# Filling a permutation array: contiguous copies inside DRAM in place of 4-byte stores from SBUF

## The chip, the cores and the metric

The kernel runs on one core of a Trainium2 chip. The metric is the device time of one execution in microseconds, the median of several runs. Engines are named as in the profile: PE (TensorE), ACT (ScalarE), DVE (VectorE), POOL (GpSimd) and SP (SyncE). SP computes nothing here; its instruction stream, written SPq in the rows, issues most of the transfers, in order.

## The reference, cut to what matters

Three layers follow each other: linear attention with decay, a layer of routed experts, and a gated feed-forward. The middle one sends each of 3072 tokens to one of 8 experts:

```python
def _moe_ref(x, w_gate, w_output_gate, w1, w2):
    logits = x @ w_gate
    e_idx = np.argmax(logits, axis=1)
    ...
    for e in range(E):
        mask = e_idx == e
        h = np.maximum(x[mask] @ w1[e], 0.0)
        ye = h @ w2[e]
        out[mask] = gate_w[mask, None] * eom[mask, e, None] * ye
    return out.astype(np.float32)

def _moe2_ref(x, w_gate, w_val, w_out, rms_g):
    rms = np.sqrt(np.mean(x * x, axis=-1, keepdims=True) + 1e-06)
    xn = x / rms * rms_g
    g = xn @ w_gate
    silu = g * (1.0 / (1.0 + np.exp(-g)))
    val = xn @ w_val
    return (silu * val @ w_out).astype(np.float32)
```

Tokens are 512 wide, the experts' hidden width is 1024, that of the feed-forward 1536. `moe_w_output_gate` is scaled by 3.472.

## The kernel before, in words

**Attention and routing** go over 24 chunks of 128 tokens. For each token POOL writes its number with an indirect transfer into the DRAM array `lst`, which has a region of 3072 places for each expert (`place`, L577). The finished rows go to `xr` in DRAM.

**Experts.** The 8 experts are handled as 8 windows, in an order that the device works out from the counts. Window `w` takes up to `CAPS[w]` tokens (448, 456, 432, 416, 408, 400, 384, 368). Its list is read from `lst` into the SBUF tile `ix` as 128-partition columns and a remainder (`load_list`, L248 and L250). POOL gathers the rows by it into `xw` (L255), TensorE transposes them (`turn`, L271), and they are split into two parts that single passes carry, `xh` and `xl`. Eight steps `f` follow: `up` (L287) makes 128 hidden units; ACT writes them as `hh` (L293) and DVE what is left of them as `hl` (L294); one step later `down` (L300) adds their product to the output. The list, the gather and the transposes of window `w + 1` run inside window `w`.

**Weights** come in 64 tiles of 512 KB, one for each step of each window. SP loads a tile into one of three `raw` buffers (L183), ACT converts it (L179) and POOL writes the remainder (L180). The conversion runs up to 9 steps ahead of use, the load two tiles ahead of the conversion, from a table that is known only once the routing is done. The order on each engine is the order of the code: a manual schedule with no planner behind it.

**Permutation.** The rows of a window are computed side by side, so their results lie in the order of the windows in `z_dram`, of which there are two, so that the first blocks of the feed-forward can start before the last windows are done. Beside each of them stands an array `p_dram` with the token's number for each place. `ids` (L278, L280) fills it: in step 0 of window `w`, SP stores the columns of `ix` and the remainder, 4 bytes at a time, into array 0 and 1 for the first four windows (`both`) and into array 1 alone after that. A window writes `CAPS[w]` places; the next window overwrites what was too much, so the order of the stores matters. Two stores into the same array wait for each other. `load_perm` (L737) reads array 0 and array 1 back in the last window.

**Feed-forward.** In the last window SP also reads the first block of 384 columns from `z_dram` (L728), and weights `raw<-wm` (L205), which ACT and DVE decode from 64-bit words (L219 to L232). Twelve steps for each pair of blocks follow (`gate`, `project`), and POOL scatters the finished rows to the output by the permutation (L778).

Of the kernel before, what the change touches and what calls it, by code (L numbers as in the profile page):

```python
# [19 lines left out]
NT, DM = B * S, H * D  # L20
# [83 lines left out]
def fused_kernel(  # L104
# [26 lines left out]

# [1 line left out]
    stage = ctx.enter_context(ExitStack())  # L133
# [29 lines left out]

# [1 line left out]
    def wslot(t):  # L165
# [70 lines left out]

# [1 line left out]
    class Experts:  # L238
        """One window: up to n tokens of one expert."""

# [32 lines left out]

        def ids(self, w, n, pos, which):
            nt, rem = divmod(n, 128)
            t = ix[w % 2]
            for i in which:
                SP.dma_start(out=p_dram[i][bass.ds(pos, nt * 128)].rearrange("(t p) o -> p t o", p=128), in_=t[:, 0:nt])  # L278
                if rem:
                    SP.dma_start(out=p_dram[i][bass.ds(pos + nt * 128, rem)], in_=t[0:rem, nt])  # L280

# [31 lines left out]
        def evac_weighted(self, w, n):  # L313
            """The squares taken on the way, and the gain applied already."""
            self.ys = self.ys2[w % len(self.ys2)]
            for k in range(KB):
                p, y, g = ps[:, 4 + k, 0:n], self.ys[:, k, 0:n], gcol[:, k:k + 1]
                if k % 2:
                    DVE.tensor_scalar(out=y, in0=p, scalar1=g, scalar2=None, op0=ALU.mult)
                ACT.activation(out=self.sq[k][:, 0:n], in_=p, func=AF.Square)  # L320
                if k % 2 == 0:
                    ACT.activation(out=y, in_=p, func=AF.Copy, scale=g)  # L322
# [34 lines left out]
    regs = {}  # L357

    def wrow(w):
        if w == 0:  # L360
            return 0
        return SP.value_load(tab[0:1, TB_ROW + w:TB_ROW + w + 1], min_val=0, max_val=NE * NT - NT)

# [16 lines left out]
    def totals_c(room):  # L380
        """Where the windows' columns begin, and what of an expert's tokens is past its window."""
        nw = tf(TB_N)
# [22 lines left out]
        DVE.tensor_tensor(out=tabf[:, TB_FLAG:TB_FLAG + 1], in0=fl[:, 0:1], in1=fl[:, 1:2], op=ALU.add)  # L405
        # where a window leaves columns unwritten, the blocks read the first window's; they are redone at the end
        DVE.scalar_tensor_tensor(
# [4 lines left out]

# [1 line left out]
    with ExitStack() as es:  # L414
# [302 lines left out]

# [1 line left out]
    def w2(f, part, s, lo, hi):  # L719
# [79 lines left out]
    def settle(w, f, bank):  # L799
        """What is left of window w once its products are done, a step at a time."""  # L800
        n = CAPS[w]
        if f == 0:
            ex.square(0, n)
            ex.square(1, n)
        elif f == 1:
            ex.square(2, n)
            ex.square(3, n)
            ex.add(1, n, DVE)
        elif f == 2:
            ex.add(2, n, DVE)  # L810
            ex.add(3, n, DVE)
        elif f == 3:
            ex.halve(w, n, DVE)
        elif f == 4:
            ex.mean(w, n, bank)
            ex.inverse(0, n // 2)
        elif f == 5:
            ex.inverse(n // 2, n)
        elif f >= 6:
            for k in range(KB):  # L820
                if f == (6 + k // 2 if w < NE - 2 else 7):
                    ex.scale(k, n)

    for w in range(NE):
        n = CAPS[w]
        for f in range(NF):
# [7 lines left out]
            if w + 1 < NE:  # L834
                if f == 0:
                    ex.load_list(w + 1, CAPS[w + 1], wrow(w + 1))
                    if w == 0:
                        ex.load_list(0, n, 0)
                    ex.ids(w, n, wpos(w), both(w))
                elif f == 1:  # L840
                    ex.gather(w + 1, CAPS[w + 1])
                    if w == 0:
                        totals_c(sq[1][0:1])
                elif f in (5, 6):
                    ex.turn(w + 1, CAPS[w + 1], (2 * (f - 5), 2 * (f - 5) + 1))
            else:
                if f == 0:
                    ex.ids(w, n, wpos(w), both(w))
                    z_block(0, 0)
# [4 lines left out]
                elif f == 6:  # L854
                    load_perm(1, 0, NT // 128)
                    z_split(1, POOL)
            if w:
                settle(w - 1, f, 2 + f % 2)
# [5 lines left out]

    # the first two blocks of the feed-forward take over while the last window settles
    w = NE - 1
# [70 lines left out]

    # the last two blocks end apart, so that what the first returns is on its way before the second ends
    b0, b1 = NB - 2, NB - 1
# [16 lines left out]

# [1 line left out]
    def within(v, most):  # L958
# [11 lines left out]
    with tc.If(flag > 0):  # L970
        with ExitStack() as es:
# [5 lines left out]
            with tc.For_i(0, NE, 1) as w:  # L977
                pieces = nc.values_load(tab[0:1, bass.ds(w + TB_K, 1)], min_val=0, max_val=MAXP)
                with tc.For_i(0, pieces, 1) as i:
# [6 lines left out]
                    ex.turn(0, PIECE, range(KB))  # L986
                    ex.ids(0, PIECE, pos, (1,))
                    for f in range(NF):
# [78 lines left out]
```

## Time and profile before

| what | value |
|---|---|
| three runs | 1172.06, 1172.99 and 4084.11 us; median 1172.99 us |
| profiled execution, span from the first to the last instruction | 1170.0 us (the page gives no time of its own beside it) |
| TensorE busy, mean granted clock | 1070.0 us (91%), 0.968 |
| DVE, ACT, POOL busy | 538.5, 381.8, 338.9 us |
| transfers | 116.74 MB, of 53405 packets 18507 under 512 B |

The experts run from about 173 to 537 us; ahead of them lies attention, behind them the feed-forward. The clock of TensorE is given as a share of full speed: 1.00 is 2.4 GHz, 0.50 is 1.2 GHz. The third run is far from the other two, and the median does not rest on it.

### The profile page before, as it was taken

The page shows a single profiled execution, that of the slowest core. Times are in us where ns is not written, and L with a number is a line of the kernel's source. Part 1 is how long each engine was busy: PE and PEld are TensorE (multiplying, and loading weights), DVE is VectorE, ACT ScalarE, POOL GpSimd, SP SyncE. Part 2 cuts the span into 40 slices and gives each one's busy share as a digit, 9 for nine tenths or more (in the row PEclk, how much of TensorE's full clock was granted, in tenths as well). Part 3 has the DMA queues.
Part 4 walks back from the last instruction along what each step waited for, and adds up shares of the span by engine and source line. Part 5 has one row for each costly group of instructions (what it writes and reads, how often), then busy time and mean ns, then how long its engine had stood idle before and what let it go on. Part 6 is the DMA issues. An engine that isn't in the chain of part 4 may idle for free.

```text
span 1170.0 us, 16406 instructions
## 1 busy us (share of the span) xinstructions
PE 1070.0 (91%) x6393; PEld 993.8 (85%) x6394; DVE 538.5 (46%) x1045; ACT 381.8 (33%) x721; POOL 338.9 (29%) x271
## 2 busy tenths in 40 slices
PE   7787885979888999978989999999999999999996
PEld 6687765868788999978878889999999999999995
DVE  4699941235345556669888872111221112211111
ACT  1344430524324445445555542111221112211111
POOL 2355521644444656633343322000020000200002
PEclk9899978889998999989999999999999999999998
DMA  8999516452736656463334322000020000200001
GB/s 293 242 322 262 159 55 70 126 120 55 217 75 179 199 170 140 134 188 100 103 102 146 126 72 82 1 1 1 13 96 1 1 1 1 83 1 1 1 1 57
DMA packets 53405, 116.74 MB, mean 100 GB/s; under 512 B 18507, under 2 KB 30027, under 8 KB 50503
## 3 DMA queue, kind: packets, MB, share of 16 engines
q1 hardware_dynamic: 45142, 97.05, 28.6%
q0 software_dynamic: 4864, 12.53, 4.9%
q10 hardware_dynamic: 3312, 6.03, 1.5%
q8 instruction: 52, 0.85, 0.3%
q14 instruction: 35, 0.28, 0.1%
HBM read 93.04 MB, written 23.11 MB: 99 GB/s over the span
## 4 chain that ended last, share of the span: by engine, by line
issue 44%; DMA 12%; PE 12%; DVE 11%; POOL 5%; ACT 2%; SPq 2%; POOLq 0%; DVEq 0%; ACTq 0%
PE ps L300 5%; PE ps L287 5%; DMA raw<-wmoe 5%; DMA perm<-ix 4%; POOL w L180 3%; DVE fb L226 2%; DVE fb L229 2%; POOL out_dram L778 2%; DVE fu L232 1%; DVE fb L223 1%; DMA raw<-wm 1%; DMA out_dram<-ob,perm 1%; DVE a L753 1%; DVE al L755 1%; ACT ah L754 1%
## 5 line engine op out<-in xcount | busy, mean ns | idle before, releaser
L745 PE MATMUL ps<-zh,w 128*128 128x384 f32 x960 | 255.7, 337 | 1.3 <-ACT a L752 1.3
L753 DVE TENSOR_TENSOR a<-a,ps 128x384 f32<-128x384 f32 x96 | 52.9, 551 | 320.1 <-PE ps L745 315.5
L180 POOL TENSOR_TENSOR w<-raw,w 128x1024 fp32r<-128x1024 f32 x64 | 156.5, 2454 | 147.6 <-ACT w L179 146.8
L745 PEld LDWEIGHTS ps<-zh,w 128*128 128x128 f32 x960 | 175.3, 188 | 4.1 <-ACT a L752 1.7
L745 PE MATMUL ps<-xh,w 128*128 128x384 f32 x576 | 156.5, 341 | 9.9 <-ACT a L752 7.3
L745 PE MATMUL ps<-zl,w 128*128 128x384 f32 x480 | 161.6, 337 | 0.0
L300 PE MATMUL ps<-hh,w 128*128 128x448 f32 (+7 forms) x512 | 114.2, 368 | 40.4 <-ACT hh L293 40.4
L287 PE MATMUL ps<-xh,w 128*128 128x448 f32 (+7 forms) x512 | 150.9, 356 | 0.1
L763 PE MATMUL ps<-w,ah 128*128 128x512 f32 x564 | 145.4, 393 | 0.2 <-ACT ys L322 0.2
L300 PEld LDWEIGHTS ps<-hh,w 128*128 128x128 f32 x512 | 98.5, 199 | 46.2 <-ACT hh L293 42.9
L778 POOL DMA_INDIRECT out_dram<-xw,perm x10 | 9.9, 994 | 423.3 <-ACT xw L776 420.0
L745 PEld LDWEIGHTS ps<-xh,w 128*128 128x128 f32 x576 | 104.9, 188 | 17.4 <-ACT a L752 11.4
L763 PEld LDWEIGHTS ps<-w,ah 128*128 128x128 f32 x564 | 104.7, 188 | 16.6 <-ACT ys L322 0.6
L754 ACT ACTIVATE ah<-a 128x384 fp32r<-128x384 f32 x94 | 49.4, 525 | 209.9 <-DVE a L753 209.9
L752 ACT ACTIVATE a<-ps 128x384 f32<-128x384 f32 x96 | 46.8, 488 | 202.2 <-PE ps L745 202.2
L179 ACT ACTIVATE w<-raw 128x1024 fp32r<-128x1024 f32 x64 | 67.4, 1056 | 101.0 <-DMA raw<-wmoe 97.7
L287 PEld LDWEIGHTS ps<-xh,w 128*128 128x128 f32 x512 | 96.5, 190 | 3.6
L294 DVE SCALAR_TENSOR_TENSOR hl<-ps,hh 128x448 fp32r<-128x448 f32 (+7 forms) x64 | 37.5, 585 | 133.2 <-ACT hh L293 133.0
L745 PE MATMUL ps<-xl,w 128*128 128x384 f32 x288 | 96.9, 336 | 0.0
L745 PEld LDWEIGHTS ps<-zl,w 128*128 128x128 f32 x480 | 90.4, 188 | 2.3
L287 PE MATMUL ps<-xl,w 128*128 128x448 f32 (+7 forms) x256 | 90.4, 353 | 0.0
L180 POOL TENSOR_TENSOR w<-fu,w 128x512 fp32r<-128x512 f32 x36 | 55.8, 1549 | 111.3 <-ACT w L179 107.8
(154 smaller groups left out, 1520.8 us busy)
## 6 DMA issues: line engine op xcount, KB each, us to landing
raw<-wmoe SPq DMA_DIRECT2D x64, 512.0 KB
qkv<-att SPq DMA_DIRECT2D x22, 1024.0 KB
raw<-wm SPq DMA_DIRECT2D x36, 512.0 KB
xw<-z SPq DMA_DIRECT2D x8, 768.0 KB
xr<-row ACTq DMA_DIRECT2D x23, 256.0 KB
z<-ys SPq DMA_DIRECT2D x2, 912.0 KB
z<-ys SPq DMA_DIRECT2D x2, 896.0 KB
z<-ys SPq DMA_DIRECT2D x2, 864.0 KB
```

The lines of the kernel that those rows point to most:

```text
L179: ACT.activation(out=dst[:, 0, c], in_=src, func=AF.Copy)
L180: POOL.tensor_tensor(out=dst[:, 1, c], in0=src, in1=f32(dst[:, 0, c]), op=ALU.subtract)
L226: DVE.scalar_tensor_tensor(out=b, in0=lo, scalar=29, in1=b, op0=ALU.logical_shift_right, op1=ALU.bitwise_or)
L287: PE.matmul(p, lhsT=wtile[:, s, k * 128:(k + 1) * 128], rhs=x[w % len(xh)][:, k, 0:n], start=(i == 0), stop=(i == 3 * KB - 1),)
L294: DVE.scalar_tensor_tensor(out=hl, in0=p, scalar=0.0, in1=f32(hh), op0=ALU.max, op1=ALU.subtract)
L300: PE.matmul(ps[:, 4 + k, 0:n], lhsT=wtile[:, s, 512 + k * 128:512 + (k + 1) * 128], rhs=h, start=(f == 0 and j == 0), stop=(f == NF - 1 an ...
L745: PE.matmul(ps[:, part, 0:BT], lhsT=w2(f, part, s, k * 128, (k + 1) * 128), rhs=zz[:, k], start=(i == 0), stop=(i == 3 * KB - 1),)
L752: ACT.activation(out=a, in_=ps[:, 0, 0:BT], func=AF.Silu)
L753: DVE.tensor_tensor(out=a, in0=a, in1=ps[:, 1, 0:BT], op=ALU.mult)
L754: ACT.activation(out=ah, in_=a, func=AF.Copy)
L763: PE.matmul(ps[:, o_bank[b % 2][t]], lhsT=x[:, t * 128:(t + 1) * 128], rhs=w2(f, 2, s, 0, 512), start=(f == 0 and j == 0), stop=(f == NF2 ...
L778: ins = POOL.indirect_dma_start(out=out[:, :], out_offset=bass.IndirectOffsetOnAxis(ap=pm[:, t0 + t], axis=0), in_=o, in_offset=None, boun ...
```

## The change

`ids` no longer stores the SBUF tile. It copies `CAPS[w]` consecutive entries from the expert's region of `lst` to the permutation array, DRAM to DRAM, as one transfer. The call moves from step 0 of the window to step 3 (array 0) and step 5 (array 1). The second reading of window 0's list, which only the old store needed, is dropped. The row offset of a window is read from the table once and kept.

```diff
-        def ids(self, w, n, pos, which):
-            nt, rem = divmod(n, 128)
-            t = ix[w % 2]
-            for i in which:
-                SP.dma_start(out=p_dram[i][bass.ds(pos, nt * 128)].rearrange("(t p) o -> p t o", p=128), in_=t[:, 0:nt])
-                if rem:
-                    SP.dma_start(out=p_dram[i][bass.ds(pos + nt * 128, rem)], in_=t[0:rem, nt])
+        def ids(self, n, row0, pos, i):
+
+            SP.dma_start(
+                out=p_dram[i][bass.ds(pos, n)].rearrange("t o -> o t"), in_=lst[bass.ds(row0, n)].rearrange("t o -> o t")
+            )
...
+    rows_at = {}
+
     def wrow(w):
         if w == 0:
             return 0
-        return SP.value_load(tab[0:1, TB_ROW + w:TB_ROW + w + 1], min_val=0, max_val=NE * NT - NT)
+        if w not in rows_at:
+            rows_at[w] = SP.value_load(tab[0:1, TB_ROW + w:TB_ROW + w + 1], min_val=0, max_val=NE * NT - NT)
+        return rows_at[w]
...
                     ex.load_list(w + 1, CAPS[w + 1], wrow(w + 1))
-                    if w == 0:
-                        ex.load_list(0, n, 0)
-                    ex.ids(w, n, wpos(w), both(w))
...
                 if f == 0:
-                    ex.ids(w, n, wpos(w), both(w))
                     z_block(0, 0)
...
+            if f in (3, 5) and f // 4 in both(w):
+                ex.ids(n, wrow(w), wpos(w), f // 4)
```

The same call in the code for other shares of the experts, which does not run with these inputs, changes alike. PE, ACT, DVE and POOL keep their instructions and order; SP's stream goes from 469 to 447 rows.

SP's stream before, second window, step 0, after the two list loads. `perm_61` and `perm_62` are the two arrays in DRAM, `ix_102` the window's list, `raw_70` a weight buffer; `DMAHW` names are counters of landed transfers.

```order
L368 TENSOR_LOAD tab [waits DVE_49]
L368 ISA x2
L278 REGISTER_ALU
L278 DMA perm_61<-ix_102 128x3x1
L280 ISA
L280 DMA perm_61<-ix_102 72x1 [waits DMAHW2_49]
L278 REGISTER_ALU
L278 DMA perm_62<-ix_102 128x3x1
L280 ISA
L280 DMA perm_62<-ix_102 72x1 [waits DMAHW5_49,DMAHW4_49]
L183 ISA
L183 DMA raw_70<-wmoe 128x1024 [waits DMAHW6_49,Pool_49]
```

The same place after: the weight loads of steps 0 to 2 follow the list loads at once; these rows begin with the last of them.

```order
L183 DMA raw_69<-wmoe 128x1024 [waits DMAHW3_49,Pool_49]
L370 TENSOR_LOAD tab [waits DVE_49]
L370 ISA x2
L276 ISA
L276 DMA perm_61<-lst 12x38
L183 ISA
L183 DMA raw_70<-wmoe 128x1024 [waits DMAHW6_49,Pool_49]
L183 ISA
L183 DMA raw_68<-wmoe 128x1024 [waits DMAHW7_49,Pool_49]
L276 ISA
L276 DMA perm_62<-lst 12x38 [waits DMAHW4_49]
```

The four stores, two of which wait for the one before, have become two copies with weight loads ahead of and between them.

SP's stream before, last window, steps 0 and 1: the store, then the first block `z_59` of the feed-forward, a result store (`ys`) and three loads of feed-forward weights.

```order
L278 REGISTER_ALU
L278 DMA perm_62<-ix_102 128x2x1
L280 ISA
L280 DMA perm_62<-ix_102 112x1 [waits DMAHW5_49,DMAHW4_49]
L728 DMA xw<-z_59 128x4x384 [waits DMASW4_49,DMASW3_49,DMASW5_49,DMASW2_49,PE_49]
L355 REGISTER_ALU
L355 DMA z_60<-ys_1994 512x1x400 [waits DVE_49]
L205 DMA raw_69<-wm 128x1024 [waits DMAHW1_49,Pool_49]
L205 DMA raw_70<-wm 128x1024 [waits DMAHW2_49,Pool_49]
L205 DMA raw_68<-wm 128x1024 [waits DMAHW3_49,Pool_49]
```

The same place after, from the last load of expert weights on.

```order
L183 DMA raw_68<-wmoe 128x1024 [waits DMAHW3_49,Pool_49]
L730 DMA xw<-z_59 128x4x384 [waits DMASW4_49,DMASW5_49,DMASW3_49,DMAHW0_49,DMASW2_49,PE_49]
L353 REGISTER_ALU
L353 DMA z_60<-ys_1994 512x1x400 [waits DVE_49]
L205 DMA raw_69<-wm 128x1024 [waits DMAHW4_49,Pool_49]
L205 DMA raw_70<-wm 128x1024 [waits DMAHW6_49,Pool_49]
L205 DMA raw_68<-wm 128x1024 [waits DMAHW7_49,Pool_49]
```

The store has left this place. It stands, as a copy, at step 5 of the window, ahead of the full read of array 1 (`perm_104<-perm_62`):

```order
L370 TENSOR_LOAD tab
L370 ISA x2
L276 ISA
L276 DMA perm_62<-lst 16x23
L205 DMA raw_69<-wm 128x1024 [waits DMAHW7_49,DVE_49,Activation_49]
L739 DMA perm_104<-perm_62 128x24x1 [waits DMAHW2_49]
L205 DMA raw_70<-wm 128x1024 [waits DMAHW0_49,DMAHW5_49,DVE_49,Activation_49]
```

Before, seven loads of feed-forward weights and four other transfers stood between the store and that read; now one load does.

## Rows read from the trace of the kernel before

**Rows 1.** The page: span, busy time by engine, and the chain that ended last by line.

```profile
span 1170.0 us, 16406 instructions
...
PE 1070.0 (91%) x6393; PEld 993.8 (85%) x6394; DVE 538.5 (46%) x1045; ACT 381.8 (33%) x721; POOL 338.9 (29%) x271
...
PE ps L300 5%; PE ps L287 5%; DMA raw<-wmoe 5%; DMA perm<-ix 4%; POOL w L180 3%; DVE fb L226 2%; DVE fb L229 2%; POOL out_dram L778 2%; DVE fu L232 1%; DVE fb L223 1%; DMA raw<-wm 1%; DMA out_dram<-ob,perm 1%; DVE a L753 1%; DVE al L755 1%; ACT ah L754 1%
```

**Rows 2.** TensorE's waits from 170 to 600 us: who waited for whom, us, times, longest.

```profile
PE ps L300 <- ACT hh L293: 40.4, 7, 13.7
PE ps L300 <- DVE hl L294: 4.1, 3, 2.3
```

**Rows 3.** TensorE's timeline: start us, us, instruction, [idle before it, releaser].

```profile
206.47 3.35 PE L300 MATMUL ps<-hh,w 128*128 128x448 f32 x8 [13.68 <-ACT hh L293]
...
253.58 3.41 PE L300 MATMUL ps<-hh,w 128*128 128x456 f32 x8 [8.38 <-ACT hh L293]
...
303.82 3.25 PE L300 MATMUL ps<-hh,w 128*128 128x432 f32 x8 [5.10 <-ACT hh L293]
...
352.82 3.14 PE L300 MATMUL ps<-hh,w 128*128 128x416 f32 x8 [5.89 <-ACT hh L293]
...
511.03 2.82 PE L300 MATMUL ps<-hh,w 128*128 128x368 f32 x8 [4.81 <-ACT hh L293]
```

**Rows 4.** ACT's timeline in the second window, same columns.

```profile
252.03 1.06 ACT L179 ACTIVATE w<-raw 128x1024 fp32r<-128x1024 f32 x1 [15.29 <-DMA raw<-wmoe]
```

**Rows 5.** SyncE's queue (SPq) in the second window: start us, us, issue.

```profile
226.41 0.43 SPq L278 DMA_DIRECT2D perm<-ix  x1
...
235.59 0.39 SPq L278 DMA_DIRECT2D perm<-ix  x1
...
245.54 29.32 SPq L183 DMA_DIRECT2D raw<-wmoe  x8
```

**Rows 6.** The waits of SyncE's queue from 170 to 500 us.

```profile
SPq L280 <- DMA perm<-ix: 69.2, 9, 8.8
```

**Rows 7.** SyncE's queue in the fifth window.

```profile
378.16 0.42 SPq L278 DMA_DIRECT2D perm<-ix  x1
385.97 0.36 SPq L280 DMA_DIRECT2D perm<-ix  x1
```

**Rows 8.** Busy us by engine in the fifth window, TensorE's granted clock, DMA share, GB/s.

```profile
377.80:416.30 38.50, 38.50 (x210) 37.52 (x209) 21.24 (x24) 17.21 (x29) 23.81 (x12) 1.00 0.54 174
```

**Rows 9.** The same view of five stretches, each right after an idle of TensorE.

```profile
206.47:211.60 5.13, 5.13 (x14) 4.58 (x15) 1.23 (x2) 2.39 (x3) 5.13 (x3) 0.50 0.30 117
253.58:259.40 5.82, 5.82 (x15) 5.11 (x16) 5.68 (x5) 2.12 (x4) 4.68 (x2) 0.50 0.44 143
303.82:307.20 3.38, 3.38 (x9) 3.14 (x10) 3.10 (x3) 0.00 (x0) 1.98 (x1) 0.50 1.04 404
352.82:358.40 5.58, 5.58 (x16) 5.33 (x17) 3.10 (x3) 0.00 (x0) 2.03 (x1) 0.50 1.08 272
511.03:515.40 4.37, 4.37 (x14) 4.37 (x15) 4.23 (x6) 4.21 (x9) 3.93 (x4) 0.50 0.04 1
```

**Rows 10.** SyncE's queue at the start of the first window.

```profile
178.86 1.60 SPq L248 DMA_DIRECT2D ix<-lst  x1
...
185.73 38.21 SPq L183 DMA_DIRECT2D raw<-wmoe  x9
```

**Rows 11.** The rings from 182 to 206 us in 40 slices.

```profile
GB/s 0 1 36 34 34 0 0 34 109 27 34 0 20 1 21 62 27 21 34 48 7 7 21 55 7 89 27 21 61 68 41 185 314 423 376 365 342 232 218 287
```

**Rows 12.** SyncE's queue in the last window.

```profile
492.92 0.64 SPq L728 DMA_DIRECT2D xw<-z  x1
...
496.25 2.12 SPq L205 DMA_DIRECT2D raw<-wm  x3
...
517.30 11.12 SPq L205 DMA_DIRECT2D raw<-wm  x4
```

**Rows 13.** ACT's timeline in the last window.

```profile
509.19 0.67 ACT L219 ACTIVATE fu<-raw 128x512 f32<-128x512 int32 x1 [9.69 <-DMA raw<-wm]
```

More of the change, by code (lines that the diff above doesn't have):

```diff
@@ L986, in fused_kernel @@
                     ex.turn(0, PIECE, range(KB))
-                    ex.ids(0, PIECE, pos, (1,))
+                    ex.ids(PIECE, within(row - i * PIECE, NE * NT - PIECE), pos, 1)
                     for f in range(NF):
```

## The prediction, made before the changed kernel was run

> **What bounds the kernel now.** I read the page first. TensorE is busy 91% of the span [rows 1], so a gain can only come from its idle stretches and from stretches at half clock. The chain that ended last gives 4% of the span to `perm<-ix`, the stores that the change replaces, and 5% to `raw<-wmoe`, the weight loads [rows 1]: 4% of 1170 is some 47 us. A share of a chain is not yet a gain, so the second view is the list of TensorE's waits between 170 and 600 us. It names one large releaser: the down products (L300) waited 40.4 us in 7 waits for ACT's `hh`, and 4.1 us in 3 waits for DVE's `hl` [rows 2]. TensorE's timeline shows where: 13.68, 8.38, 5.10 and 5.89 us in the first four windows (a window is one expert's turn) and 4.81 us in the last [rows 3]; the two waits of the seven that have no row are 40.4 - 37.86 = 2.5 us, and they follow the third and fourth. So the first four windows lose 40.4 - 4.81 = 35.6 us to idling.
>
> The third view, ACT's timeline, says why `hh` is late. ACT runs in order, and ahead of `hh` stands the conversion of a weight tile (L179), which sat idle 15.29 us for the load `raw<-wmoe` [rows 4]. The tile converted there is used several steps later: TensorE does not lack weights, it stands behind an ACT that stands behind a load. The fourth view, the queue of SyncE, says why the load is late. In the second window SP issued the first array's store at 226.41, the second's at 235.59 and the next weight load at 245.54 [rows 5]: 19.1 us in which no load went out. The wait is at L280: the remainder's store waits until the main store has landed, 69.2 us in 9 waits, 7.7 us each and 8.8 at most [rows 6].
>
> The control is in the same trace. From the fifth window on only one array is stored, so SP stands still once: 378.16 to 385.97 [rows 7]. In that window TensorE is busy 38.50 of 38.50 us at full clock [rows 8]. A block of 7.8 us costs nothing; one of 19.1 us costs 8.38. The slack of a load, two tiles ahead, thus lies between 7.8 and 19.1 - 8.38 = 10.7 us.
>
> **The change part by part.** *Stores removed.* Windows 0 to 3 lose both blocks on SP. What is left there in a row is two list loads of some 0.4 us of issue each, and the weight loads behind them. All 35.6 us of idling hang on loads behind the blocks, so I count them whole. Each idle stretch is followed by one at a granted clock of 0.50, which is the 1.2 GHz level: 5.13, 5.82, 3.38 and 5.58 us in the four windows [rows 9]. Work there takes twice its time, so half is lost: 19.91 / 2 = 10.0 us. It comes back if the idle before it goes, because stretches without idle hold 1.00 [rows 8]. Together 45.6 us.
>
> *First window.* Here the loads start only after the routing table is known. They went out from 185.73 on [rows 10], and from 182 to 206 us the rings moved 109 GB/s or less in the first 31 of 40 slices and 185 to 423 only in the last nine [rows 11]; in that stretch were the gather and three loads, 512 KB each, beside stores of 4 bytes. The second reading of the first list and the four stores fill the queue from 178.86 to the first load [rows 10]; both go, and the loads can go out about 6 us sooner. The gather (456 rows of 2 KB, 0.9 MB) and three loads (1.5 MB) are 2.4 MB, some 7 us at 350 GB/s, about what most of those last slices show. From 180 that ends near 187 to 190, and TensorE's idling began at 206.47 - 13.68 = 192.8 [rows 3]. I leave 1.5 us of idling in place; the bounds are 0 and the whole 13.68 + 5.13 / 2 = 16.2 us.
>
> *Copies added.* Twelve copies of 1.5 to 1.8 KB, at steps 3 and 5, each with one issue. No store of this shape is in the trace; the bounds for its landing are 0.4 us (an issue alone) and the old store's 8.8 [rows 6]. I take 2 to 3 us: 1.5 KB in 7.7 us is 0.2 GB/s on rings that also show over 300 [rows 11], so it was not the bytes that took long, and where the old store had several hundred pieces of 4 bytes the copy has 12 or 16 of 92 to 152. It is no term of the sum, since in windows 0 to 6 nothing that follows soon waits for it: the next copy into the same array comes a window later, some 40 us, and the loads behind it read other memory. Cover gone (8.8 us, and the queue stopped for it), the slack of 7.8 to 10.7 us still takes it, one copy at a time. SP's issue of a copy is like that of a store, and 12 replace 23.
>
> *Last window.* The first store of the window goes, so the read of the first feed-forward block, issued at 492.92 [rows 12], no longer stands behind it. It can go as soon as the last transposes have read the buffer, near 488. A result store that waits for DVE still stands ahead of the first load of feed-forward weights, issued at 496.25 [rows 12]; this does not move against TensorE. But ACT, idle for that load, began on it only at 509.19 [rows 13], because the block's 768 KB, the store's 800 KB and 4-byte reads shared the rings with it. With the block's read done before, it lands some 5 us sooner or more, and the stall was 4.81 us. I take all of that and of its half-clock stretch: 4.81 + 4.37 / 2 = 7.0 us [rows 3, 9]. The upper bound adds the 4.1 us of waits for `hl` [rows 2], 11.1 in all; the lower is 0, since DVE's decoding of the weights (L223 to L232) comes next as the limit and could hold TensorE as long.
>
> *The wait that is added.* The full read of the second array (L737) now follows the last window's copy with one weight load between them. That load is the last of a run of four that took 11.12 us from 517.30 on, waiting for buffers [rows 12], so the copy has several us of cover; price 0. With an 8.8 us landing it would hold SP, and the weight loads queued behind, at most 5 us.
>
> Sum: 45.6 - 1.5 + 7.0 = 51.1 us off. The profiled span is 1170.0 us [rows 1], which gives 1118.9. The median of the runs shown is 2.99 us above the span, which I take to lie around it: **1122 us**. Bounds of this case: 45.6 + 11.1 = 56.7 off is 1116; 45.6 - 1.5 + 0 = 44.1 off is 1129.
>
> **The rivals.** *The copies land as slowly as the stores did.* Their pieces are still small, and the target is the same array. Then the last window gains nothing (7.0) and in the first window the loads again share the rings with slow writes (half of 16.2, 8.1): 1122 + 15 = 1137. For it speaks that no row shows a faster write of this kind; against it, that there are 28 times fewer of them (16 for 448). The Trainium skill has a rule that speaks for this rival: "DMA: Bandwidth & Descriptors", section Specifications, puts the minimum for line rate at 512 B and says that below it the engine reads, modifies and writes. The copies' pieces are below it as the old ones were. The same page (Anatomy of one DMA) gives a fixed cost of about 2.0 us, mostly the receipt of the write; by that figure a 1.5 KB store would land in an estimated 2 us, where the trace has 7.7 [rows 6], so on this point the trace does not agree, and by the page alone the copies would cost nothing at all and the sum would stay.
>
> *The first window keeps its stall.* Its loads begin only when the table is read, and the gather competes. If the late start and not the stores is the cause, 13.68 + 2.57 - 1.5 = 14.8 us stay: 1137. Against it: 182 to 206 us moved little in most slices [rows 11]; rings that were full of real work would show 300 GB/s throughout.
>
> *The stall moves to the result stores.* In windows 2 and 3 two result stores stand in the queue just ahead of the loads. If these are the cause there, 5.10 + 5.89 + 2.5 idling and 4.5 of clock stay, 18 us: 1140. Window 4 has the same two stores, after a block, and no idle [rows 7, 8].
>
> *Slower: the copies run as single 4-byte elements* from DRAM to DRAM, and each holds the rings for long. A load behind one then lands L us late, and TensorE idles by L less the slack of 10.7, plus about 2.5 us of clock. Twelve copies eat the gain of 51 when 12 x (L - 10.7 + 2.5) exceeds it, from L = 12.5 on. At L = 16, twice the old store, the loss is 12 x 7.8 = 94 against 51: 1216. Against it: the built program gives each copy as 12 or 16 pieces.
>
> **How the numbers follow.** Forecast 0.72, slow landing 0.12 and first window 0.11 (both near 1137), result stores 0.02, slower 0.03. The range runs from a little under the best bound, 1113, to 1138, which takes in the forecast's case and about half of the spread of the two at 1137; some 0.16 stay outside. A change under 2% (23.5 us, about what a measurement here can tell from none) means a time between 1149.5 and 1196.5. The first four cases all lie under that, with a little of their spread above: faster 0.95, same 0.02, slower 0.03.
>
> **What would show it.** In the new profile: no wait of SP at the copies; no idle of the down products behind `hh` in windows 1 to 3 and at most 3 us in window 0; clock 1.00 from about 173 us to the last window; windows 0 to 3 some 12 us shorter each on average; the first feed-forward load landing within 8 us of its issue. The prediction is wrong if ACT still idles for `raw<-wmoe` for over 10 us after the stores are gone, or if the gained time comes back as waits for DVE in the stage after the last window.

## The result, and the profile after

The changed kernel took 1118.99 us (median of four runs, 1117.51 to 1120.68), the kernel before 1172.53 in the same comparison (four runs, one of them the 4084.11 of the first table): a ratio of 0.9549, interval 0.9534 to 0.9563. The forecast was 1122, with a range of 1113 to 1138. The profiled execution took 1119.29 us, 2.1 us more than its span of 1117.2.

The page of the changed kernel, the lines that answer to [rows 1]:

```profile
span 1117.2 us, 16379 instructions
...
PE 1055.5 (94%) x6393; PEld 982.8 (88%) x6394; DVE 550.9 (49%) x1045; ACT 381.4 (34%) x721; POOL 337.2 (30%) x271
...
PE ps L285 12%; PE ps L298 11%; DVE fb L226 2%; DVE fb L229 2%; POOL out_dram L780 2%; DVE fu L232 1%; DVE fb L223 1%; PE ps L271 1%; DMA out_dram<-ob,perm 1%; DVE a L755 1%; DVE al L757 1%; ACT ah L756 1%; DVE ys L347 1%; PE ps L604 1%; DMA raw<-wm 1%
```

The stores to the permutation arrays (4% of the chain before) and the loads of expert weights (5%) are no longer among the lines that the page lists. In their place stand the products of the experts, 12% and 11% where they had 5% each: in the experts' stage the chain now runs through TensorE itself.

TensorE's waits in the changed kernel from 170 to 600 us, against [rows 2]; up and down products are now at lines 285 and 298:

```profile
PE ps L747 <- ACT a L754: 4.5, 6, 0.9
PE ps L298 <- DVE hl L292: 4.4, 3, 2.3
...
PE ps L747 <- DVE hl L292: 1.3, 1, 1.3
```

The 40.4 us behind ACT's `hh` have no entry left, here or in the rows left out. The waits for DVE's `hl` at the down products are what they were, 4.4 against 4.1 us, and one wait of 1.3 us for `hl` has appeared among the first feed-forward products.

The link between the loads and TensorE is ACT. Its waits for expert weights from 170 to 500 us, before and after:

```profile
ACT w L179 <- DMA raw<-wmoe: 97.7, 17, 21.3
```

```profile
ACT w L179 <- DMA raw<-wmoe: 0.5, 2, 0.4
```

The 97.7 us have become 0.5. TensorE from 180 us to the start of the last window in the changed kernel (the columns of [rows 8]):

```profile
180.00:445.90 265.90, 265.90 (x1417) 253.42 (x1416) 150.54 (x163) 119.38 (x187) 161.19 (x82) 1.00 0.53 165
```

It is busy in all of the 265.90 us, at a granted clock of 1.00.

SyncE's queue in the second window, against [rows 5]:

```profile
208.90 0.39 SPq L248 DMA_DIRECT2D ix<-lst  x1
209.50 0.34 SPq L250 DMA_DIRECT2D ix<-lst  x1
211.05 10.88 SPq L183 DMA_DIRECT2D raw<-wmoe  x3
222.78 0.97 SPq L276 DMA_DIRECT2D perm<-lst  x1
...
232.28 0.83 SPq L276 DMA_DIRECT2D perm<-lst  x1
```

Behind the two list loads (L248, L250) the next load goes out 1.5 us later, at 211.05, where it took 19.1 us from the first store to the next load. The two copies (L276) stand between loads. The waits of that queue from 170 to 500 us, the four largest of ten entries and the only one behind a load, against [rows 6]:

```profile
SPq L183 <- POOL w L180: 166.2, 47, 7.6
SPq L205 <- DVE fb L229: 32.4, 7, 8.6
SPq L353 <- DVE hl L292: 22.4, 5, 7.3
SPq L589 <- ACT row L588: 22.3, 1, 22.3
...
SPq L183 <- DMA raw<-wmoe: 1.4, 1, 1.4
```

None of the ten names a permutation array. What the copies took: first their issue on SyncE from the view of the tile `perm` (ns, least, median and most), then their landing from the list of transfers from 175 to 490 us (the last figure is us from issue to landing, known for three of the twelve copies):

```profile
L276 SPq DMA_DIRECT2D perm<-lst x12: 520/644/969, 181.2 to 471.5; - x12
```

```profile
perm<-lst SPq DMA_DIRECT2D x2, 1.8 KB, 4.3
...
perm<-lst SPq DMA_DIRECT2D x2, 1.7 KB, 3.1
...
perm<-lst SPq DMA_DIRECT2D x1, 1.4 KB, 2.7
```

In the last window (SyncE's queue, then ACT; against [rows 12, 13]):

```profile
441.92 0.65 SPq L730 DMA_DIRECT2D xw<-z  x1
...
450.32 2.29 SPq L205 DMA_DIRECT2D raw<-wm  x3
```

```profile
456.04 0.68 ACT L219 ACTIVATE fu<-raw 128x512 f32<-128x512 int32 x1 [2.45 <-DMA raw<-wm]
```

The block is read at 441.92, and SyncE reaches the first load of feed-forward weights 8.4 us later, held by the result store. ACT takes that tile at 456.04, 5.7 us after the issue of 450.32; before it was 509.19 - 496.25 = 12.9.

Where the time went can be read from TensorE's timelines. The experts, from the first up product (173.0 before, 173.3 after) to the first feed-forward product (537.3 and 484.1), took 364.3 us and now take 310.7: 53.6 less. From there to the end it is 632.7 before and 633.1 after, so next to nothing was given back later. Of the 53.6, windows 0 to 3 give 46.2 (the first window alone 16.2), windows 4 to 6, which took 110.7 in both, nothing, and the last window 7.3.

### The profile page after: what moved, and what is told of

Same layout as the page of the kernel before. It is cut to its first block, busy times and chain, and to the rows that moved or that the text cites. A ratio compares the mean times of both kernels' runs of the same rounds, so it can differ in the third digit from the quotient of the medians.

```text
span 1117.2 us, 16379 instructions
## 1 busy us (share of the span) xinstructions
PE 1055.5 (94%) x6393; PEld 982.8 (88%) x6394; DVE 550.9 (49%) x1045; ACT 381.4 (34%) x721; POOL 337.2 (30%) x271
## 4 chain that ended last, share of the span: by engine, by line
issue 43%; PE 25%; DVE 11%; POOL 3%; DMA 2%; ACT 2%; POOLq 0%; DVEq 0%; SPq 0%; ACTq 0%
PE ps L285 12%; PE ps L298 11%; DVE fb L226 2%; DVE fb L229 2%; POOL out_dram L780 2%; DVE fu L232 1%; DVE fb L223 1%; PE ps L271 1%; DMA out_dram<-ob,perm 1%; DVE a L755 1%; DVE al L757 1%; ACT ah L756 1%; DVE ys L347 1%; PE ps L604 1%; DMA raw<-wm 1%
## 5 line engine op out<-in xcount | busy, mean ns | idle before, releaser
L755 DVE TENSOR_TENSOR a<-a,ps 128x384 f32<-128x384 f32 x96 | 52.8, 550 | 320.2 <-PE ps L747 317.7
L298 PE MATMUL ps<-hh,w 128*128 128x448 f32 (+7 forms) x512 | 106.6, 350 | 0.0
L298 PEld LDWEIGHTS ps<-hh,w 128*128 128x128 f32 x512 | 93.8, 188 | 2.9
L765 PE MATMUL ps<-w,al 128*128 128x512 f32 x282 | 80.1, 392 | 0.0
L757 DVE TENSOR_TENSOR al<-a,ah 128x384 fp32r<-128x384 f32 x94 | 52.5, 558 | 55.5 <-ACT ah L756 55.5
```

What stands on the lines that cost most here:

```text
L298: PE.matmul(ps[:, 4 + k, 0:n], lhsT=wtile[:, s, 512 + k * 128:512 + (k + 1) * 128], rhs=h, start=(f == 0 and j == 0), stop=(f == NF - 1 an ...
L755: DVE.tensor_tensor(out=a, in0=a, in1=ps[:, 1, 0:BT], op=ALU.mult)
L757: DVE.tensor_tensor(out=al, in0=a, in1=f32(ah), op=ALU.subtract)
L765: PE.matmul(ps[:, o_bank[b % 2][t]], lhsT=x[:, t * 128:(t + 1) * 128], rhs=w2(f, 2, s, 0, 512), start=(f == 0 and j == 0), stop=(f == NF2 ...
```

## The experiments

The theories are named in the expectations: **A**, only the time for which SyncE stands still counts; **B**, 4-byte pieces drain slowly and hold what stands behind them in the rings; **C**, step 0 is the wrong place; later **D**, which joins A and B with a slack, and **E**, stores from SBUF are the slow ones. The runs were made in three sets, on chips 1 (the first four), 15 (the next four) and 5 (the last three). There the kernel before took 1180 to 1183 us where the first comparison has 1172.53, so ratios are compared, and the changed kernel itself was run again in the last set.

| run | us | ratio to before, interval |
|---|---|---|
| old stores at steps 3 and 5 | 1157.88 | 0.9778, 0.9749 to 0.9808 |
| one padded store for each array, step 0 | 1156.10 | 0.9773, 0.9745 to 0.9800 |
| change in the last window alone | 1172.86 | 0.9911, 0.9884 to 0.9939 |
| change in the first window alone | 1166.37 | 0.9842, 0.9809 to 0.9875 |
| copies split, at step 0 | 1121.61 | 0.9489, 0.9465 to 0.9513 |
| copies of single elements, steps 3 and 5 | 1122.39 | 0.9498, 0.9474 to 0.9521 |
| changed kernel and 4 copies in a row | 1121.49 | 0.9492, 0.9471 to 0.9514 |
| changed kernel and 7 copies in a row | 1149.07 | 0.9721, 0.9687 to 0.9755 |
| changed kernel again | 1122.77 | 0.9499, 0.9456 to 0.9542 |
| one padded store for each array, steps 3 and 5 | 1123.83 | 0.9523, 0.9484 to 0.9562 |
| copies of single elements, step 0 | 1154.31 | 0.9763, 0.9723 to 0.9802 |

**Old stores, moved.** In the kernel before:

```diff
-                    ex.ids(w, n, wpos(w), both(w))
...
+            if f in (3, 5) and f // 4 in both(w):
+                ex.ids(w, n, wpos(w), (f // 4,))
```

> The kernel before with its 4-byte stores left as they are, but array 0's at step 3 and array 1's at step 5 of each window. Theory A (SyncE stands still while a store lands, and only the length of one block matters): two blocks of about 7.7 us each, both under a load's slack of 7.8 to 10.7 us, so windows 0 to 3 lose their idle of 35.6 us and their half-clock loss; the last window gains between 0 and 7 us. 1120 to 1130 us. Theory B (the 4-byte pieces drain slowly and hold whatever stands behind them in the rings, wait or no wait): a load behind a store is late by the block and by the hold, so some idle of 2 to 5 us stays in each of the first windows: 1135 to 1150 us.

SyncE's queue in the second window:

```profile
232.72 0.42 SPq L278 DMA_DIRECT2D perm<-ix  x1
243.43 0.39 SPq L280 DMA_DIRECT2D perm<-ix  x1
...
245.55 0.41 SPq L278 DMA_DIRECT2D perm<-ix  x1
259.94 0.35 SPq L280 DMA_DIRECT2D perm<-ix  x1
```

The first remainder waits 10.7 us and the second 14.4, not 7.7. With weight loads ahead in the rings the stores land later, and the second block alone is longer than the slack of 7.8 to 10.7. What the rings moved from 245 to 260 us, in 40 slices:

```profile
GB/s 120 186 33 11 0 0 131 44 0 87 87 131 33 55 87 33 415 426 404 307 187 23 0 0 0 0 0 0 0 0 0 0 0 0 0 0 0 0 0 0
```

Loads fill them until 253; in the 7 us after that, until the remainder goes out at 259.94, nothing moves. TensorE's waits in that run:

```profile
PE ps L300 <- ACT hh L293: 17.4, 7, 5.5
```

Less than half of the 40.4 us; window 0 has only 0.63 and 1.68 of it. There the first two loads went out ahead of the first store, and no remainder waits in that window. In the stage after, TensorE waited 5.54 us for ACT, new in this run. As a ratio the time is what theory B expected (1135 to 1150 of 1172.99 is 0.968 to 0.980), but the waits say that SyncE's block can be part of it. Neither A with its 7.7 us nor B alone is settled by this.

**One store, no wait.** In the kernel before, lists padded to whole columns (the arrays have room for it):

```diff
-            nt, rem = divmod(n, 128)
+            nt = -(-n // 128)
...
-                if rem:
-                    SP.dma_start(out=p_dram[i][bass.ds(pos + nt * 128, rem)], in_=t[0:rem, nt])
```

> The kernel before with each list padded to whole columns of 128, so that each array takes one 4-byte store at step 0 and no store waits for another; same place, same kind of piece, 384 or 512 of them for each array. Theory A: no block on SyncE, so windows 1 to 3 lose their idle and clock loss (29.4 us); window 0, whose stores never waited for each other, keeps its stall; about 1140 us. Theory B: the weight loads go out at once but land late behind two stores' worth of 4-byte pieces, as in window 0 before, where the load issued at 185.73 was ready at 204.9; idle of 5 to 14 us stays in each of the first four windows: 1160 to 1185 us.

SyncE's queue in the second window, then the load in the chain that ended last and ACT there, then TensorE in the first two windows:

```profile
225.99 0.97 SPq L276 DMA_DIRECT2D perm<-ix  x2
227.22 38.05 SPq L183 DMA_DIRECT2D raw<-wmoe  x8
```

```profile
227.22 17.83 DMA raw<-wmoe
```

```profile
245.07 1.06 ACT L179 ACTIVATE w<-raw 128x1024 fp32r<-128x1024 f32 x1 [8.18 <-DMA raw<-wmoe]
```

```profile
206.85 3.35 PE L296 MATMUL ps<-hh,w 128*128 128x448 f32 x8 [13.90 <-ACT hh L289]
...
246.61 1.92 PE L296 MATMUL ps<-hh,w 128*128 128x456 f32 x8 [1.27 <-ACT hh L289]
```

The load goes out 1.2 us after the stores, at 227.22, and lands 17.8 us later, where the median of such loads in the changed kernel is 3.9; ACT idles 8.18 us for it until 245.07. SyncE did not hold it back, so the rings did. Nearly the same stretch of TensorE's work in this run and in the changed kernel shows how (the last two figures are the DMA engines' busy share and GB/s):

```profile
226.00:245.00 19.00, 19.00 (x94) 17.23 (x92) 4.55 (x6) 5.99 (x11) 10.06 (x7) 1.00 0.62 58
```

```profile
211.00:230.00 19.00, 19.00 (x94) 17.24 (x93) 5.81 (x9) 8.06 (x15) 12.15 (x9) 1.00 0.44 129
```

With the small pieces the DMA engines are busier and move less than half. TensorE's idle falls from 8.38 to 1.27 in the second window, stays at 4.6 and 5.0 in the third and fourth, and in window 0 it is 13.90 as before. The outcome, 0.9773, lies between A's ratio (1140 of 1172.99 is 0.972) and B's (0.989 or more): both act, the block and the rings.

**One window at a time.** The copies at steps 3 and 5 in window 0 alone, and the copy at step 5 in the last window alone, the old stores elsewhere:

```diff
+            if w == NE - 1 and f == 5:
+                ex.copy_ids(n, wrow(w), wpos(w), 1)
```

```diff
-                    if w == 0:
-                        ex.load_list(0, n, 0)
-                    ex.ids(w, n, wpos(w), both(w))
+                    if w:
+                        ex.ids(w, n, wpos(w), both(w))
...
+            if w == 0 and f in (3, 5):
+                ex.copy_ids(n, 0, 0, f // 4)
```

> The kernel before, with the change in the last window alone (copy at step 5 there in place of the stores at step 0). By the sum's term: 4.8 us of idle and 2.2 of clock go, 1165.5 us. If DVE's decoding takes over as the limit at once, 1172; if the waits for DVE's remainder go as well, 1161.

> The kernel before, with the change in window 0 alone (copies at steps 3 and 5, no second reading of the list). By the sum's term 16.2 us go less at most 1.5: 1156 to 1158 us. If the late start of the loads and the gather made that stall, it stays and the time is 1170 or more.

TensorE's waits behind `hh` in these two runs (last window, first window), and its last wait of that kind in the second:

```profile
PE ps L305 <- ACT hh L298: 41.5, 5, 13.4
```

```profile
PE ps L305 <- ACT hh L298: 33.9, 5, 11.5
```

```profile
508.62 2.82 PE L305 MATMUL ps<-hh,w 128*128 128x368 f32 x8 [6.89 <-ACT hh L298]
```

Against the kernel before in that set the last window alone is worth 1183 x 0.0089 = 10.5 us (7.2 to 13.7), the first alone 18.7 (14.8 to 22.6). The terms were 7.0 and 14.7 (16.2 at most). The last window's stall is larger in this set, 6.89 us where the first trace has 4.81. Together the two runs also give an estimate of the idle of the kernel before in this set, 41.5 + 6.89 = 48.4 us against 40.4, which is 8 of the 10.5 us by which it is slower there. With the change in the first window alone no wait behind `hh` is left in window 0. This edit also lets the loads go out earlier, so by itself it does not separate the stores from the late start. The next run does: there the first load goes out 10.6 us after the window's first product, against 6.7 in the changed kernel and 12.7 before, beside the same gather, and window 0 has no stall. The stores made it.

**Contiguous copies, in the old place and with the old waits.** In the changed kernel, both arrays at step 0, main part and remainder:

```diff
+            m = n // 128 * 128
+            for a, c in ((0, m), (m, n - m)):
+                if c:
...
+                    for i in both(w):
+                        ex.ids(n, wrow(w), wpos(w), i)
```

> The changed kernel with its copies put back to step 0 and split into a main part and a remainder, so that the remainder's copy waits for the main one as the stores did; only the kind of piece differs from before. In the changed kernel a copy lands in 2.8 us, so SyncE is blocked for some 3.4 us for each array. Theory A (length of SyncE's block): 7 us for both arrays, under the slack, no idle; ratio to before 0.955, as the changed kernel has. Theory B (4-byte pieces): no such pieces, no idle; 0.955. Theory C (the place, step 0 beside the list and the gather, was the trouble): idle of some us in each of the first four windows, 0.965 or more.

SyncE's queue in the second window:

```profile
213.65 5.94 SPq L278 DMA_DIRECT2D perm<-lst  x4
219.86 30.80 SPq L183 DMA_DIRECT2D raw<-wmoe  x8
```

The 2.8 us in the expectation were read wrongly: they are the median of a view that also holds the 24 scatters of the output, and the copies' known landings are 2.7, 3.1 and 4.3. The four copies, two of them waiting, take 6.2 us where the four stores took 19.1. No wait behind `hh` is left, and the ratio is that of the changed kernel. Place and wait are harmless if a transfer lands soon; C falls.

**Small pieces, spread.** In the changed kernel, each copy as 4-byte elements:

```diff
-                out=p_dram[i][bass.ds(pos, n)].rearrange("t o -> o t"), in_=lst[bass.ds(row0, n)].rearrange("t o -> o t")
+                out=p_dram[i][bass.ds(pos, -(-n // 128) * 128)].rearrange("(t p) o -> p t o", p=128),
+                in_=lst[bass.ds(row0, -(-n // 128) * 128)].rearrange("(t p) o -> p t o", p=128),
```

> The changed kernel, each copy laid out so that it moves 384 or 512 single elements of 4 bytes from DRAM to DRAM, at steps 3 and 5, with no wait of SyncE between them. Theory A: no block on SyncE in windows 0 to 6, so no idle there; the last window's read of the array waits for the copy and may cost up to 8 us: 0.955 to 0.963 of before. Theory B: the weight loads behind each copy land late, idle of 2 to 5 us after many of the 12 copies with half-clock loss on top: 0.97 to 0.99.

Two of SyncE's waits in it:

```profile
SPq L183 <- DMA raw<-wmoe: 7.8, 6, 2.4
...
SPq L740 <- DMA perm<-lst: 4.3, 1, 4.3
```

TensorE never waits behind `hh`. The loads do land somewhat late (SyncE waits 7.8 us in six places for an earlier load, and ACT 12.2 us in eight, 3.2 at most), and the read of the second array waits 4.3 us for its copy, but the time is the changed kernel's. B as stated falls: 384 to 512 pieces of 4 bytes, one transfer at a time and with no wait behind them, cost nothing here.

**A dose of waiting without small pieces.** Four, then seven more contiguous copies into array 1 at step 0 of windows 1 to 6, each waiting for the last:

```diff
+                    for _ in range(7 if w else 0):
+                        ex.ids(n, wrow(w), wpos(w), 1)
```

> The changed kernel with four more copies of the same list into array 1 in a row at step 0 of windows 1 to 6; each waits for the one before, and no 4-byte piece is written. Theory A: a block of 3 x 3.4 + 0.7 = 11 us on SyncE in six windows, at the edge of the slack of 7.8 to 10.7: idle of 0 to 2 us in each, 0.955 to 0.965 of before. Theory B: nothing, 0.955.

> As the run with four, but seven copies in a row. Theory A: a block of 6 x 3.4 + 0.7 = 21 us, idle of about 10 us in each of six windows with 2.5 us of clock on top, some 60 to 80 us: 1.005 to 1.025 of before. Theory B: nothing, 0.955.

SyncE's queue in the second window with four and with seven, and TensorE's waits with seven:

```profile
212.08 7.34 SPq L276 DMA_DIRECT2D perm<-lst  x4
219.69 3.66 SPq L183 DMA_DIRECT2D raw<-wmoe  x3
```

```profile
212.76 13.76 SPq L276 DMA_DIRECT2D perm<-lst  x7
226.80 1.51 SPq L183 DMA_DIRECT2D raw<-wmoe  x3
```

```profile
PE ps L298 <- ACT hh L291: 18.8, 9, 4.5
```

A copy in the row costs 1.9 to 2.0 us, not 3.4, so the blocks are 7.6 and 14.0 us here, not 11 and 21. Four copies cost nothing; seven cost 18.8 / 6 = 3.1 us of idle in a window on average, and 27.6 us in all. B, which expected nothing, fails here. The slack is not one number, though. The six blocks of seven copies last 12.2 to 14.0 us, and a block less its idle gives 14.0 - 0.8 = 13.3 in the second window and 7.6 to 11.6 in the five after it, where result stores of 0.8 to 0.9 MB follow the first load; the mean is 10.0. (The 10.9 in the expectation of a later run took the second window's block with the mean idle.) The length of the block counts even without small pieces.

**Theory D tried both ways.** The padded 4-byte stores of the second run, at steps 3 and 5, and the 4-byte copies of the sixth, both at step 0:

```diff
-                    ex.ids(w, n, wpos(w), both(w))
+            if f in (3, 5) and f // 4 in both(w):
+                ex.ids(w, n, wpos(w), (f // 4,))
```

```diff
-            if f in (3, 5) and f // 4 in both(w):
-                ex.ids(n, wrow(w), wpos(w), f // 4)
+                    for i in both(w):
+                        ex.ids(n, wrow(w), wpos(w), i)
```

> The changed kernel unaltered, beside the two others of this set. Earlier sets had the kernel before at 1182 to 1183 us where the first comparison had it at 1172.5, and split copies at step 0 at 0.949 of it: 0.948 to 0.955 of before.

> The kernel before with one padded 4-byte store for each array, as in the run with one store, but array 0's at step 3 and array 1's at step 5. Theory D (a 4-byte transfer delays the loads behind it by some 8 to 16 us, through SyncE if a wait follows it and through the rings if none does, and idle comes only past a slack of about 10.9 us): one such transfer at a time, no wait; idle of 0 to 3 us in each of the first four windows as in the run with element copies, 0.95 to 0.965 of before. Theory E (stores from SBUF are slower than copies from DRAM, whatever waits): idle as with the old stores at steps 3 and 5, 0.975 to 0.985.

> The run with single 4-byte elements copied from DRAM to DRAM, but both arrays' copies at step 0, one right behind the other, still with no wait between them. Theory D: two in a row hold the rings for longer than the slack, so idle comes back as in the run with one store at step 0, 1 to 5 us in windows 1 to 3 and over 10 us in window 0, 0.97 to 0.98 of before. Theory A (only SyncE's waits count): no idle, 0.95.

TensorE's waits, the two largest entries from 165 to 600 us, with the padded stores at steps 3 and 5:

```profile
PE ps L741 <- ACT a L748: 4.6, 6, 0.9
PE ps L296 <- DVE hl L290: 3.9, 2, 2.0
```

No entry stands behind `hh`; 0.9523, within the interval of the changed kernel in the same set, with 4-byte stores from SBUF. Against the old stores at these steps (0.9778) only the remainders and the waits for the main stores are gone. ACT still waits 20.0 us in 13 places for a load, 3.6 at most: late, but within the lead. E falls. The 4-byte copies at step 0, SyncE's queue and ACT in the second window, and TensorE's waits:

```profile
227.58 1.51 SPq L276 DMA_DIRECT2D perm<-lst  x2
229.35 43.66 SPq L183 DMA_DIRECT2D raw<-wmoe  x8
```

```profile
250.48 1.06 ACT L179 ACTIVATE w<-raw 128x1024 fp32r<-128x1024 f32 x1 [12.72 <-DMA raw<-wmoe]
```

```profile
PE ps L299 <- ACT hh L292: 24.6, 6, 8.2
```

Two in a row, no wait: the load behind them goes out at once, at 229.35, ACT idles 12.72 us for a tile, and 24.6 us of TensorE's waits are back; 0.9763. D gave the times of both runs. Its idle was off in size: 8.2 us in window 0 where it had over 10, 5.8, 4.5 and 6.1 in windows 1 to 3 where it had 1 to 5. The edit between this run and the one at steps 3 and 5 is the place alone, which also puts the two copies of a window one behind the other. Windows 4 to 6 tell these apart: there one such copy stands at step 0, and no idle follows.

## Why the prediction was right, point by point

**What bounds.** The chain from the late load over ACT's order to TensorE was right, and it accounts for the whole gain: ACT's 97.7 us of waiting for expert weights and the idle behind `hh` are gone, and the time after the experts is as before. What made the loads late was SyncE's block only in part (see the stores below).

**The slack.** 7.8 to 10.7 us was read from two windows of one trace. Four copies in a row cost nothing at 7.6, and seven gave 10.0 on average, but 13.3 in the second window, from which the 10.7 was read, and 7.6 at the least. The subtraction took SyncE's block for the whole delay; the loads behind it were late in the rings as well. That the bracket fits the mean is partly luck. A lead of this size is why two stores in one step cost so much and one in the later windows cost nothing.

**Stores removed, 45.6 us.** Right in size: windows 0 to 3 take 46.2 us less, against 45.6 less the 1.5 kept for the first window, and 1.00 is granted up to the last window. The words were too narrow, though. "Both blocks on SP" fits the second window, where the stall falls from 8.38 to 1.27 once no remainder waits. In the third and fourth 4.6 and 5.0 us stay without any such wait, half or more of the 7.0 and 9.7 that the old stores leave there in the same set (the run with the last window changed): that part is the rings. In window 0 the stores never waited for each other (the description of the kernel, by which two stores into one array wait, does not hold there), and its stall stayed at 13.90 with one store for each array; there it was the rings. The first window's part did name the rings. It took 16.2 us less, the upper bound: the 1.5 us that I left in place did not show.

**Copies at no cost.** Right in cost: no wait names them. The three landings that the trace gives are 2.7, 3.1 and 4.3 us, against a guess of 2 to 3. The runs add that this guess carried less than it seemed. At steps 3 and 5 even 4-byte pieces cost nothing, and at step 0 even split copies with their waits did not. Either half of the change, contiguous pieces or one transfer at a time at steps 3 and 5 without a wait, gives all of its gain; the old stores merely moved, with their waits, give less than half.

**Last window, 7.0 us.** The last window takes 7.3 us less. The stall of 4.81 went, the load was ready 7.2 us sooner after its issue, and the waits for `hl` stayed, as was said. By itself, in another set, it was 10.5 (7.2 to 13.7), with a stall there of 6.89.

**The added wait.** Price 0 was right, no entry names it. With slower pieces it was 4.3 us of SyncE's time and still no time of the kernel.

**The signs.** All that were named came: no wait of SyncE at the copies, no idle behind `hh`, clock 1.00 from 180 us to the last window, windows 0 to 3 shorter by 11.6 us each on average, the first feed-forward load ready 5.7 us after its issue. Neither sign of a wrong prediction did: ACT idled 0.5 us for expert weights, and the stage after the last window is about as long as before.

**The rivals.** Slow landing did not come, and it was priced too high: 15 us were set down for it, where 4-byte copies at the same steps cost nothing. The same holds for the slower case, 94 us: its mechanism was built and did no harm, since the delay of one such transfer stays under the slack (ACT waited 3.2 us at most for a load there). The result stores in windows 2 and 3 were no cause, since they still stand there and no idle does. *The first window keeps its stall* fell with the split copies at step 0. The sum of 51.1 stands against 52.8 on the span; the 1.5 us of the first window make up most of the difference. The rest of the 3 us between 1122 and 1118.99 is the median, which lay 1.8 us above the span and not 2.99.

## What to carry to other kernels

Here a load that was late by less than its lead cost nothing, and one that was late by more cost TensorE the rest and a stretch at half clock. So small transfers in the queue that also issues the loads should come one at a time, between loads, and with nothing in that queue waiting for them to land. Which window of the old kernel shows no stall, and what it does differently, gives a first bracket for the lead before anything is run; a block less its idle is not the lead where the load is also late for another reason.

## What the runs showed of the hardware

A store of some 400 entries in 4-byte pieces was waited for 7.7 us on average in the first trace, and 10.7 and 14.4 us behind weight loads in the run with the stores moved; the same entries in 12 or 16 contiguous pieces landed in 2.7, 3.1 and 4.3. The Trainium skill ("DMA: Bandwidth & Descriptors", Anatomy of one DMA) has about 2.0 us of fixed cost for a transfer, stated for transfers that GpSimd issues. The contiguous copies are nearer to that than the 4-byte store. The prediction set the figure beside a store that SyncE issues.

Moving the pieces is little of the 7.7 us. SyncE waits for a main store from 226.41 to 235.03 in the first trace, and there the rings, from 226 to 236 us in 40 slices, moved this:

```profile
GB/s 296 182 263 67 18 4 3 0 0 0 0 0 0 0 0 0 0 0 0 0 0 0 0 0 0 0 0 0 0 0 0 0 0 0 0 0 0 0 0 1
```

From about 228 on nothing moves until the remainder goes out, as in the run with the stores moved. So "drain slowly" in theory B is not what the traces show; what the landing waits for in those 7 us stays open. The same small pieces delay other transfers with no semaphore between: the load issued at 227.22 right behind two such stores landed 17.8 us later, with the DMA engines busy 0.62 of the time at 58 GB/s. A wait for a contiguous copy, in a row of seven, was 41.0 / 36 = 1.1 us beside an issue of 0.6, less than the landings that the trace of the changed kernel shows; why it is shorter there stays open. So does why the kernel before takes 8 to 10 us longer in the later sets than in the first comparison; its stalls were an estimated 8 us longer in the first of these sets, and the changed kernel differs by less than 4 us between the first comparison and the last set.
